# When loads, bank seeds and weight jobs are issued in a kernel of 518 hand-ordered steps

## The chip, the cores and the metric

The kernel runs on one core of a Trainium2 chip. The metric is the device time of one execution, in microseconds (us), the median of several runs.

## The reference

Two branches work on the same input x (2048 x 640) and are mixed by a gate. All sizes are float32.

```
g = sigmoid((x * gate_w).sum(-1))                      # one gate for each row
a, b = x @ dft_hid_re.T, x @ dft_hid_im.T              # 640 x 640 each
A = dft_seq_re @ a - dft_seq_im @ b                    # 2048 x 2048 each
h = x @ w1 + b1                                        # 640 x 1728
B = (h * tanh(softplus(h))) @ w2                       # Mish, then 1728 x 640
out = g * A + (1 - g) * B
```

## The kernel before, in words

**Arithmetic.** Every float32 operand is split into two rounded parts: ScalarE copies it to the high part (`rh` for moving operands, `wh` for weights), VectorE subtracts to get the low part (`rl`, `wl`). A product is three matmuls, high by high, high by low, low by high (`mm3`, all recorded at line 141; splits at line 125 for the copies of ScalarE and line 122 for the sums of VectorE). Blocks of 2 x 2 are multiplied with seven products in place of eight (Strassen-Winograd), so that many sums of operands, of weights and of results lie on VectorE, and partial results pass through DRAM or are copied back into a PSUM bank as the start of another sum. Such a copy is called a *seed* here (`preload`, `seed`, `take_y`: ScalarE `ps<-f`).

**Steps.** All the work of TensorE is cut into 518 steps, each of 6 to 25 matmuls of 128 x 512, in one list, `steps`: raw loads, preparations (`prep`: splits), matmuls, and a `post` that takes results out of the banks. In order they are: the stages on the sequence and the hidden dimension (steps 0 to 335), the dense stage x @ w1 (336 to 417) and the out stage with w2 (418 to 517). The dense stage begins at step `nd` = 336 with four pairs of remainder steps `r` (`dense_rest`, the last block of columns) and seven quad steps `q` (`dense_quads(0)`, one block of a second level of seven products) in an order written out by hand, `ORDER`; then `dense_first(0)` from `nm` = 351, `dense_quads(1)` from `nq` = 379, and `dense_first(1)` to step 417. A pair of column groups f, f+1 in `dense_first` takes steps p5, p6, p3, p7 and p4 for both: p5 opens bank "b", p6 adds to bank "a", into which a partial product that an earlier quad had stored to DRAM (`p1_...`) was loaded and seeded; p3 ends with a product of the odd column block, operand "dd", a difference of two tiles.

**One loop sets the order of everything** (lines 1346 to 1393). All engines but SP run their own queue in program order. For each step i the loop emits: the preparations of steps up to i + LEAD_D (6, in the dense stage; 7 elsewhere), and before them raw loads of steps up to AHEAD_D (6) further; step i's matmuls; stores that are due; step i's `post`; the events that were attached to step i with `at`; pieces of weight jobs; loads for further weight jobs. All loads and stores go through the one queue of SP, in this order; an entry that waits holds up those behind it. A raw load is issued early only while more than `spare(i)` buffers are free.

**Weight jobs** (splitting and summing blocks of weights, the gate rows, sums of x) stand in one list; `JOBS` gives its last part. A job's pieces are emitted after a step when a planner's account of VectorE's time is behind that of TensorE:

```
1385  while clock["dve"] < clock["pe"] + (SLACK_D if nd <= i < nm + D_END else SLACK if ("seq", "low", KH - 1) in done_jobs else SLACK_UP) and i >= wait_until and i not in quiet:
```

So SLACK_D (0.0) holds from step 336 up to nm + D_END, SLACK (-1.0) before and after it, in us. In the `quiet` steps (nd - 4 to nd + QUIET and nm - 7 to nm + QUIET_M) no piece is emitted, in the `no_load` steps (three before the out stage to NO_LOAD after its start) no job's loads. `need(key)` in a preparation forces all pieces up to that job at once. `XS_FIRST` and `FIRSTS` give the first step at which certain jobs may be loaded.

**Seeds.** `P_SEED`, `P_SEED_0`: the event, counted from its pair's p5, at which `dense_first` seeds a bank "a" (`_0`: the first pair of the first call); `P_LOAD`, `P_LOAD_0`: how many steps ahead its tile is loaded. `SEED_Q` and `P_Q_0`: the same for the banks of `dense_quads(1)`. `take_y` (line 638): the out stage's first banks are seeded with a negative partial y, in an event one step before that stage's step n, from a tile loaded at n - 6. `T0`: steps, counted from nm, to which the loads of operands s1, s2, s4, dd, s3 of `dense_first(0)` are attached; their split is prepared LEAD_D steps ahead of that. `E_LEAD` and `R1` place the splits of narrow operands of the quads and of a remainder step.

Of the kernel before, what the change touches and what calls it, by code (L numbers as in the profile page):

```python
# [23 lines left out]
EARLY = 3  # L24
LEAD = 7
LEAD_D = 6
AHEAD_D = 6
AHEAD = 6
SPARE = 3
SPARE_D = 2  # L30
SPARE_OUT = 5
SLACK = -1.0
SLACK_UP = 2.5
SLACK_D = 0.0
QUIET = 2
NR = 9
NFS = 22
NFX = 4
# [3 lines left out]
BACK = -17  # L42
NB = 3
NLOAD = 6
QUIET_M = -3
D_END = 7
ORDER = 'rrqrrqrrqqrqrqq'
Q_LEAD = 2
P_Q = 2
P_LOAD = 4  # L50
P_LOAD_0 = 3
P_SEED = 0
P_SEED_0 = -1
P3_LAG = 2
Q_LAG = 0
SEED_Q = 1
P_Q_0 = 4
NO_LOAD = 5
XS_FIRST = 179
XS_EACH = 8  # L60
T0 = (0, 5, 5, 8, 6)
T1 = (3, 3, 5, 5, 7, 10, 10)
QX_AT = -1
N_KEPT = 1
Q2_LEAD = 1
E_LEAD = 2
R0 = (3, 2)
R1 = (1, 3)
JOBS = 'q0 q1 q2 y20 y21 y22 y23 y24 y30 y31 t2 y32 y33 t3 y34 l0 t1 l1 t0 l2 t4 t5 c r l3 l4 l5'
FIRSTS = {'y20': 37, 'y34': 42, 'l0': 22, 't2': 0}  # L70

# [14 lines left out]
def fnet_mish_gate(ctx: ExitStack, tc: tile.TileContext, xn, xt, c_re, c_im, wd_re, wd_im,  # L88
# [35 lines left out]
    def copy(o, a, scale=1.0):  # L124
        nc.scalar.activation(o, a, AF.Copy, scale=scale)  # L125
# [38 lines left out]
    def at(i, fn):  # L164

        events.setdefault(i, []).append(fn)
# [14 lines left out]
    def simple(fn):  # L181
        def work(*a):
            fn(*a)
            return
            yield
        return work
# [6 lines left out]
    def fs_load(src):  # L193
        f = FS.get()
        nc.sync.dma_start(f[:src.shape[0]], src)
        return f
# [171 lines left out]
    class Problem:  # L368
# [269 lines left out]
        def take_y(self, name, t, d, n):  # L638

            at(n - 6, lambda: RAW.update({("y", d): fs_load(ysc[d][t])}))  # L640

            def put():
                f, ps = RAW.pop(("y", d)), psum.get()
                PS.setdefault(name, []).append(ps)
                copy(ps, f, -1.0)
                FS.put(f)
            at(n - 1, put)

        def y_load(self, i, t, *ds):
            for d in ds:  # L650
# [135 lines left out]
    def w2_job(name, g):  # L786
        W2C[name] = W.get()
        split(*W2C[name], g)
        FX.put(g)
# [19 lines left out]
    def x_split(key, f, keep=False):  # L809
        r = X[key] = R.get()  # L810
        split(r[0], r[1], f)
        if not keep:
            FS.put(f)
# [6 lines left out]
    def x_diff(key, a, b):  # L820
        f, g = RAW.pop(a), RAW.pop(b)
        tt(f, f, g, OP.subtract)
        FS.put(g)
        x_split(key, f)
# [87 lines left out]
    def x_sums(dst, a21, a22, a11, a12):  # L912
        s1 = FS.get()
        tt(s1, a21, a22, OP.add)
        store(dst("s1"), s1, s1)
        yield 1
        tt(a21, a11, a21, OP.subtract)
        store(dst("s3"), a21, a21)
        FS.put(a11)
        yield 1  # L920
        tt(a22, a22, a21, OP.subtract)
        store(dst("s2"), a22, a22)
        yield 1
        tt(a12, a12, a22, OP.subtract)
        store(dst("s4"), a12, a12)

    def x_sum_jobs():
# [3 lines left out]
        for n, (key, dst, srcs) in enumerate(todo):  # L931
            jobs.append(Job(key, lambda *f, dst=dst: x_sums(dst, *f), lambda srcs=srcs: [fs_load(v) for v in srcs], fs=5))
            jobs[-1].first = XS_FIRST + XS_EACH * n

# [22 lines left out]
    def dense_quads(q):  # L957
# [64 lines left out]
        def p1_loads(n, j, tp):  # L1022
            def go():
                for g in range(FP // 2):
                    assert id(qout[2 * g + j][tp]) not in unwritten
                    KEEP["c", 2 * g + j, tp] = fs_load(qout[2 * g + j][tp])
            at(n, go)
            takes[n] = takes.get(n, 0) + 3

        for b, x, w, d, post in (("b", "a12", "b21", (0, "d1", 0), lambda: snap("b", "q2")),  # L1030
# [19 lines left out]
            if x == "a12":  # L1050
                preps = [lambda: [need(k) for k in ["five"] * q + [("quad", q, g) for g in range(FP // 2)]]]
                if q:
                    at(n - SEED_Q, seed)
                    p1_loads(n - P_Q_0, 0, 0)
                    narrow_loads.extend((n + E_LEAD + i, (("xe", t), xt[t, KD - 1])) for t, i in ((0, 0), (2, 2)))
                    attach.append((n + E_LEAD, lambda: x_split(("d1", 0, 0), RAW[("xe", 0)], True)))
                    attach.append((n + E_LEAD + 2, lambda: x_split(("d1", 0, 1), RAW[("xe", 2)], True)))
                    attach.append((n + E_LEAD + 4, lambda: x_diff(("de", 0, 0), ("xe", 0), ("xe", 2))))
            if q and x in ("s1", "s2", "a22"):
# [8 lines left out]
    def dense_first(tp, end, ops):  # L1068
# [39 lines left out]
        def p1_load(f):  # L1108
            assert id(qout[f][tp]) not in unwritten
            KEEP["p1", f] = fs_load(qout[f][tp])  # L1110

        def seed(f):

            H["a", f] = psum.get()
            p1 = KEEP.pop(("p1", f))
            copy(H["a", f], p1)
            FS.put(p1)
# [9 lines left out]
        def parts(fp):  # L1127

            fa, fb, over = fp, fp + FP, fp == FP - 1

            def free(*names):
                if over:
                    x_free(*[(n, k, tp) for n in names for k in range(2 if n[0] != "d" else 1)])

            def p5_post():
                snap("p5", "b", fp)
                free("s1")

            def p6_post():
                snap("u2", "a", fp)  # L1140
                free("s2")

            def p3_post():
                o = add("b", "u2", fp)
                pop("b", fp)
                later(P3_LAG, lambda: out_act(fb, t1, o, o))
                free("s4", "dd")

            def p7_post():
                o = add("a", "p5", fp)  # L1150
                at(clock["step"] + 1, lambda: out_act(fb, t2, o, o))
                free("s3")

            def p4_post():
                ps = H.pop(("a", fp))

                def last():
                    out_act(fa, t2, FS.get(), ps)
                    psum.put(ps)
                at(clock["step"] + 2, last)  # L1160
                free("a22", "d2")
                if end:
                    W.put(*W1[fp])
                    if fp == FP - 1:
                        W.put(*T2B, *W5)

            return [
                ([lambda: need(("w1", fp))], sub(fp, [("b", "s1", at_cols(1, 0), True)], [("b", "d2", 1)]), p5_post),
                ([], sub(fp, [("a", "s2", t2_at(fp), False)]), p6_post),
                ([], sub(fp, [("b", "s4", at_cols(0, 2 * P), False)], [("b", "dd", 1)]), p3_post),  # L1170
                ([], sub(fp, [("a", "s3", at_cols(1, 2 * P), False)]), p7_post),
                ([], sub(fp, [("a", "a22", at_cols(0, 0), False)], [("a", "d2", 0)]), p4_post)]


        for fp in range(0, FP, 2):
            for j in range(2):
                f, n = fp + j, len(steps) + j
                if True:
                    i = n - (P_LOAD if tp or fp else P_LOAD_0)
                    at(i, lambda f=f: p1_load(f))  # L1180
                    takes[i] = takes.get(i, 0) + 1
                at(n + (P_SEED if tp or fp else P_SEED_0), lambda f=f: seed(f))
            p5, p6, p3, p7, p4 = zip(parts(fp), parts(fp + 1))
# [92 lines left out]

    for o in JOBS.split():
        if o[0] == "y":
# [7 lines left out]
        else:  # L1286
            jobs.append(Job("w2r", simple(lambda g: w2_job("r", g)), w2r_load, 1, 1))
        if o in FIRSTS:
            first_at[jobs[-1].key] = FIRSTS[o]
    sq[0].first(True)  # L1290
# [12 lines left out]
    nd = len(steps)  # L1303
    rests = [dense_rest(2, False, (0, 0)), dense_rest(3, False, (0, 0)), dense_rest(0, True, R0), dense_rest(1, True, R1, True)]
    rests = [r for r in rests for _ in range(2)]
    quads = dense_quads(0)
    for o in ORDER:
        next(quads if o == "q" else rests.pop(0))
    n0 = nm = len(steps)
    dense_first(0, False, [("s1", n0 + T0[0]), ("s2", n0 + T0[1]), ("s4", n0 + T0[2]), ("dd", n0 + T0[3]), ("s3", n0 + T0[4])])  # L1310
    nq = len(steps)
# [8 lines left out]
    narrow.update(range(nd, len(steps)))  # L1320
    quiet = set(range(nd - 4, nd + QUIET)) | set(range(nm - 7, nm + QUIET_M))
    n_dense = len(steps)
    no_load = set(range(n_dense - 3, n_dense + NO_LOAD))
    ou[0].first(ks=range(3))
# [16 lines left out]
    def spare(i, job=False):  # L1341

        return SPARE + (SPARE_D * job if i in narrow else (i >= n_dense) * SPARE_OUT) + sum(takes.get(i + j, 0) for j in range(5))

    li = ready = 0
    wait_until = 0
    for i in range(n_all):
        clock["step"] = i
        while ready < n_all and ready <= i + (LEAD_D if ready in narrow else LEAD):
            while li < len(loads) and loads[li][0] <= ready + (AHEAD_D if loads[li][0] in narrow else AHEAD):  # L1350
                n, (key, src) = loads[li]
# [30 lines left out]
        if not (jobs or loaded or running):  # L1382
            while FX.free:
                FS.put(FX.get()[:, :N])
        while clock["dve"] < clock["pe"] + (SLACK_D if nd <= i < nm + D_END else SLACK if ("seq", "low", KH - 1) in done_jobs else SLACK_UP) and i >= wait_until and i not in quiet:
            if running:
# [55 lines left out]
```

## Time and profile before

| | us |
|---|---|
| median of three runs | 863.79 (863.53 to 863.9) |
| the profiled execution | 863.96 |
| its span in the profile | 862.2 |
| TensorE busy (3757 matmuls) | 855.5 |
| VectorE busy | 739.1 |
| ScalarE busy | 501.6 |

Times in the profile count from the start of the span. PE is TensorE, PEld its weight loads, DVE VectorE, ACT ScalarE, SP (or SPq) the queue of DMA issues. A row of a timeline has the start, the duration, engine, line, operation, tiles written and read, their size and the number of instructions put together; in brackets stands how long the engine had been idle before and what released it. The duration of a matmul is modelled and overlaps the next one's, so the distance from start to start is what counts. A row of the windows has the stretch, its length, TensorE's busy time with its count of matmuls, the granted clock (1.00 is full), the share of DMA time and GB/s. A row of the chain has start, length, and what the last instruction of all was waiting for at that time, followed back.

### The profile page before, as it was taken

The page shows a single profiled execution, that of the slowest core. Times are in us where ns is not written, and L with a number is a line of the kernel's source. Part 1 is how long each engine was busy: PE and PEld are TensorE (multiplying, and loading weights), DVE is VectorE, ACT ScalarE, POOL GpSimd, SP SyncE. Part 2 cuts the span into 40 slices and gives each one's busy share as a digit, 9 for nine tenths or more (in the row PEclk, how much of TensorE's full clock was granted, in tenths as well). Part 3 has the DMA queues.
Part 4 walks back from the last instruction along what each step waited for, and adds up shares of the span by engine and source line. Part 5 has one row for each costly group of instructions (what it writes and reads, how often), then busy time and mean ns, then how long its engine had stood idle before and what let it go on. Part 6 is the DMA issues. An engine that isn't in the chain of part 4 may idle for free.

```text
span 862.2 us, 12400 instructions
## 1 busy us (share of the span) xinstructions
PE 855.5 (99%) x3757; PEld 706.1 (82%) x3757; DVE 739.1 (86%) x1296; ACT 501.6 (58%) x933; POOL 0.2 (0%) x4
## 2 busy tenths in 40 slices
PE   9999999999999999999999999999999999999998
PEld 7888888888888888888888888778888887888886
DVE  6999988889879779898998996956877988998993
ACT  6756645464554544657656766857865857442532
POOL 0000000000000000000000000000000000000000
PEclk9999999999999999999999999999999999999999
DMA  9976748786859899989586979787999997595952
GB/s 349 327 239 229 258 132 307 276 278 217 298 202 296 277 353 310 367 262 361 194 264 201 329 247 346 272 277 226 342 326 381 333 367 234 191 318 174 348 194 109
DMA packets 130915, 237.35 MB, mean 275 GB/s; under 512 B 15008, under 2 KB 19872, under 8 KB 130848
## 3 DMA queue, kind: packets, MB, share of 16 engines
q1 hardware_dynamic: 130416, 235.91, 79.7%
q8 instruction: 29, 0.48, 0.2%
q10 hardware_dynamic: 432, 0.66, 0.2%
q14 instruction: 38, 0.31, 0.1%
HBM read 186.16 MB, written 50.35 MB: 274 GB/s over the span
## 4 chain that ended last, share of the span: by engine, by line
PE 94%; DVE 2%; ACT 2%; DMA 1%; issue 1%; SPq 0%; DVEq 0%
PE ps L141 94%; DVE f L122 1%; ACT f L125 1%; ACT wh L125 1%; DMA p<-f 1%; DVE rl L122 1%; DVE wl L122 1%; DMA act<-f 0%; DMA f<-p 0%; ACT rh L125 0%; ACT f L831 0%; DVE f L874 0%; DVE fx L122 0%; ACT ps L125 0%; ACT f L879 0%
## 5 line engine op out<-in xcount | busy, mean ns | idle before, releaser
L141 PE MATMUL ps<-rh,wh 128*128 128x512 f32 (+1 forms) x1067 | 414.3, 390 | 0.7 <-ACT ps L125 0.5
L141 PE MATMUL ps<-rh,wl 128*128 128x512 f32 x1051 | 408.0, 389 | 0.0
L141 PE MATMUL ps<-rl,wh 128*128 128x512 f32 x1050 | 407.6, 389 | 0.0
L125 ACT ACTIVATE rh<-f 128x512 fp32r<-128x512 f32 (+1 forms) x427 | 256.0, 626 | 181.4 <-DVE f L122 87.7
L122 DVE TENSOR_TENSOR rl<-f,rh 128x512 fp32r<-128x512 f32 x425 | 277.8, 685 | 52.7 <-ACT rh L125 45.6
L141 PEld LDWEIGHTS ps<-rh,wh 128*128 128x128 f32 x1067 | 200.4, 188 | 43.3 <-ACT ps L125 0.9
L122 DVE TENSOR_TENSOR f<-f,f 128x512 f32<-128x512 f32 (+1 forms) x337 | 225.3, 674 | 9.1 <-ACT f L125 1.3
L141 PEld LDWEIGHTS ps<-rh,wl 128*128 128x128 f32 x1051 | 197.3, 188 | 41.1
L141 PEld LDWEIGHTS ps<-rl,wh 128*128 128x128 f32 x1050 | 197.1, 188 | 40.7
L125 ACT ACTIVATE f<-ps 128x512 f32<-128x512 f32 (+1 forms) x153 | 88.6, 594 | 73.8 <-PE ps L141 68.4
L125 ACT ACTIVATE wh<-f 128x512 fp32r<-128x512 f32 (+3 forms) x188 | 85.3, 495 | 52.4 <-DVE f L122 49.2
L122 DVE TENSOR_TENSOR wl<-f,wh 128x512 fp32r<-128x512 f32 (+3 forms) x188 | 92.7, 526 | 20.5 <-ACT wh L125 20.1
L141 PE MATMUL ps<-wh,wh 128*128 128x512 f32 x197 | 77.0, 391 | 1.3 <-ACT wh L125 1.2
L141 PE MATMUL ps<-wl,wh 128*128 128x512 f32 x192 | 74.8, 390 | 0.2 <-DVE wl L122 0.2
L141 PE MATMUL ps<-wh,wl 128*128 128x512 f32 x191 | 74.4, 389 | 0.0
L122 DVE TENSOR_TENSOR f<-ps,f 128x512 f32<-128x512 f32 x83 | 53.8, 681 | 13.3 <-PE ps L141 13.2
L141 PEld LDWEIGHTS ps<-wh,wh 128*128 128x128 f32 x197 | 37.0, 188 | 10.1 <-ACT wh L125 2.0
L141 PEld LDWEIGHTS ps<-wl,wh 128*128 128x128 f32 x192 | 36.0, 188 | 7.9 <-DVE wl L122 0.5
L141 PEld LDWEIGHTS ps<-wh,wl 128*128 128x128 f32 x191 | 35.9, 188 | 7.4
L125 ACT ACTIVATE ps<-f 128x512 f32<-128x512 f32 x49 | 27.7, 594 | 17.7 <-DVE f L122 12.9
L122 DVE TENSOR_TENSOR wl<-fx,wh 128x640 fp32r<-128x640 f32 (+4 forms) x44 | 28.5, 654 | 6.6 <-ACT wh L125 6.6
L831 ACT ACTIVATE f<-f,b1s 128x512 f32<-128x512 f32 x36 | 24.5, 716 | 13.0 <-DVE f L122 13.0
(37 smaller groups left out, 167.5 us busy)
## 6 DMA issues: line engine op xcount, KB each, us to landing
f<-in_c_re_dram SPq DMA_DIRECT2D x128, 256.0 KB, 4.5
f<-in_c_im_dram SPq DMA_DIRECT2D x128, 256.0 KB, 4.7
f<-act SPq DMA_DIRECT2D x94, 256.0 KB, 5.1
f<-u SPq DMA_DIRECT2D x80, 256.0 KB, 4.4
f<-in_xt_dram SPq DMA_DIRECT2D x59, 256.0 KB, 5.1
act<-f SPq DMA_DIRECT2D x52, 256.0 KB, 5.1
u<-f SPq DMA_DIRECT2D x40, 256.0 KB, 4.3
f<-y SPq DMA_DIRECT2D x34, 256.0 KB, 5.3
```

The costliest lines, as they stand in the source:

```text
L122: nc.vector.tensor_tensor(o, a, b, op=op)
L125: nc.scalar.activation(o, a, AF.Copy, scale=scale)
L141: nc.tensor.matmul(ps, a, b, start=start, stop=stop, skip_group_check=True)
L831: nc.scalar.activation(o[rows], src[rows], AF.Mish, bias=b1s[rows, f:f + 1])
```

## The change

No operation is added or taken away; constants that place things are changed, and `take_y` gets one of its own.

- AHEAD_D: raw loads of the dense stage three steps ahead of their preparation, not six. SPARE_OUT: one buffer less is kept free in the out stage.
- SLACK -1.5 and not -1.0, QUIET, QUIET_M, D_END: the weight jobs' budget and the steps without pieces; the stretch in which SLACK_D holds ends before step nm - 1 = 350 and not before nm + 7 = 358; the first quiet stretch ends before nd - 3 and not before nd + 2, the second before nm - 2 and not before nm - 3.
- ORDER: the last remainder pair's second step comes ahead of quad step s4, not behind it. Before, steps 346 to 350 are r, q (s4), r, q (s3), q (a22); after, r, r, q (s4), q (s3), q (a22).
- P_LOAD 3 (was 4), P_SEED_0 0 (was -1): tiles of `dense_first` are loaded three steps ahead; its first pair of banks is seeded one event later.
- Y_SEED 2: `take_y` seeds two steps ahead of its stage, not one. SEED_Q 3 (was 1) and P_Q_0 7 (was 4): the second quad's seeds and their loads, two and three steps earlier.
- T0's last 8 (was 6): operand s3 two steps later, behind dd. E_LEAD 1, R1 (1, 4): a narrow split one step earlier, half of a remainder operand's split one step later.
- NO_LOAD, XS_FIRST, FIRSTS, JOBS: loads of jobs sooner after the out stage's start; sums of x 16 steps earlier; `l0` 8 steps earlier; t2 and t3 further ahead in the list, l3 last.

```diff
-AHEAD_D = 6
+AHEAD_D = 3
-SPARE_OUT = 5
-SLACK = -1.0
+SPARE_OUT = 4
+SLACK = -1.5
-QUIET = 2
+QUIET = -3
-QUIET_M = -3
-D_END = 7
-ORDER = 'rrqrrqrrqqrqrqq'
+QUIET_M = -2
+D_END = -1
+ORDER = 'rrqrrqrrqqrrqqq'
-P_LOAD = 4
+P_LOAD = 3
-P_SEED_0 = -1
+P_SEED_0 = 0
-SEED_Q = 1
-P_Q_0 = 4
-NO_LOAD = 5
-XS_FIRST = 179
+Y_SEED = 2
+SEED_Q = 3
+P_Q_0 = 7
+NO_LOAD = 1
+XS_FIRST = 163
-T0 = (0, 5, 5, 8, 6)
+T0 = (0, 5, 5, 8, 8)
-E_LEAD = 2
+E_LEAD = 1
-R1 = (1, 3)
-JOBS = 'q0 q1 q2 y20 y21 y22 y23 y24 y30 y31 t2 y32 y33 t3 y34 l0 t1 l1 t0 l2 t4 t5 c r l3 l4 l5'
-FIRSTS = {'y20': 37, 'y34': 42, 'l0': 22, 't2': 0}
+R1 = (1, 4)
+JOBS = 'q0 q1 q2 y20 y21 y22 t2 y23 y24 y30 y31 y32 t3 y33 y34 l0 t1 l1 t0 l2 t4 t5 c r l4 l5 l3'
+FIRSTS = {'y20': 37, 'y34': 42, 'l0': 14, 't2': 0}
...
-            at(n - 1, put)
+            at(n - Y_SEED, put)
```

## The prediction

> **What bounds the kernel now.** I read the page first, then the windows of TensorE, the chain, and around each piece of the chain that is not TensorE the timeline.
>
> ```profile
> span 862.2 us, 12400 instructions
> ...
> PE 855.5 (99%) x3757; PEld 706.1 (82%) x3757; DVE 739.1 (86%) x1296; ACT 501.6 (58%) x933; POOL 0.2 (0%) x4
> ...
> ```
>
> TensorE is busy 99% of the span. Busy is a modelled figure, so the pitch decides: how far apart matmuls start where nothing stops them.
>
> ```profile
> 568.00:683.00 115.00, 115.00 (x509) 1.00 0.89 309
> ```
>
> 509 matmuls in 115.0 us are 0.226 us each at a granted clock of 1.00. The program issues the same 3757 matmuls after the change, so 0.226 us each is the floor, and only what makes TensorE stand still can be won. The Trainium skill, page "TensorE: Matmul & The Clock Gate", section "Back-to-back issue gap", gives about 131 ns for a sustained matmul of 512 columns; by that, matmuls would need some 492 us (an estimate) and VectorE would set the time. This trace does not agree: 226 ns.
>
> ```profile
> 554.11 5.37 DMA p<-f
> ...
> 559.54 2.76 DMA f<-p
> ...
> 567.20 108.24 PE ps L141 x476
> ...
> 713.12 145.37 PE ps L141 x640
> ```
>
> In the chain the last 145 us are TensorE alone. What lies before it shows where the stream broke; the starts of TensorE's matmuls give all five places with a pitch over 0.24 us after the first microseconds:
>
> ```profile
> 554.03 0.39 PE L141 MATMUL ps<-rh,wl 128*128 128x512 f32 x1
> 555.17 0.47 PE L141 MATMUL ps<-wh,wh 128*128 128x512 f32 x1 [0.75 <-ACT wh L125]
> 555.48 0.40 PE L141 MATMUL ps<-wl,wh 128*128 128x512 f32 x1
> ...
> 562.51 0.39 PE L141 MATMUL ps<-wh,wl 128*128 128x512 f32 x1
> 562.98 0.50 PE L141 MATMUL ps<-wh,wh 128*128 128x512 f32 x1
> ...
> 565.62 0.39 PE L141 MATMUL ps<-rh,wl 128*128 128x512 f32 x1
> 566.47 0.50 PE L141 MATMUL ps<-wh,wh 128*128 128x512 f32 x1 [0.46 <-ACT wh L125]
> 567.20 0.50 PE L141 MATMUL ps<-wl,wh 128*128 128x512 f32 x1 [0.22 <-DVE wl L122]
> 567.53 0.40 PE L141 MATMUL ps<-wh,wl 128*128 128x512 f32 x1
> ...
> 683.20 0.39 PE L141 MATMUL ps<-wh,wl 128*128 128x512 f32 x1
> 683.75 0.50 PE L141 MATMUL ps<-rh,wh 128*128 128x512 f32 x1 [0.16 <-DVE f L122]
> ...
> 712.23 0.39 PE L141 MATMUL ps<-rh,wl 128*128 128x512 f32 x1
> 713.12 0.50 PE L141 MATMUL ps<-rh,wh 128*128 128x512 f32 x1 [0.50 <-ACT ps L125]
> ```
>
> Loss is the distance of starts less 0.226 per matmul. **S1** (step 350, last of the first quad's): 1.45 - 0.45 = 1.0 us, with the slower restart (0.31) in it. **S2** (step 354): 0.47 - 0.23 = 0.24, and 0.1 for a restart as in S1 and S3: 0.35. **S3** (the dd products of step 355): 1.91 - 0.68 = 1.23. **S4** (step 416): 0.55 - 0.23 + 0.1 = 0.42. **S5** (step 430): 0.89 - 0.23 + 0.1 = 0.76. Together 3.76 us, 0.44% of the time. No edit can win more; whatever it does elsewhere is hidden beside TensorE or costs.
>
> **The change part by part.** All engines issue the same instructions; only their order changes.
>
> **S1.** Step 350 writes the bank that step 349 filled, and waits for VectorE's sum out of it.
>
> ```profile
> 550.30 1.21 DVE L122 TENSOR_TENSOR wl<-f,wh 128x128 fp32r<-128x128 f32 x3
> 551.43 1.88 DVE L122 TENSOR_TENSOR f<-ps,f 128x512 f32<-128x512 f32 x3
> ...
> 552.42 0.60 ACT L125 ACTIVATE f<-ps 64x512 f32<-64x512 f32 x1 [1.06 <-PE ps L141]
> ...
> 553.23 0.73 DVE L874 SCALAR_TENSOR_TENSOR f<-ps,b1s,f 64x512 f32<-64x512 f32 x1
> ...
> 554.35 1.87 DVE L122 TENSOR_TENSOR f<-ps,f 128x512 f32<-128x512 f32 x3
> ```
>
> The first of the three sums at 554.35 ends at 555.02 (1.87 less two pitches of 0.6), and TensorE goes on at 555.17. VectorE is late because the remainder step's copy (552.42) and its addition (553.23) come just before, behind weight pieces (550.30) that a `need` forced. ORDER puts the remainder step ahead of quad s4 (steps 347 and 348 change places): its copy then starts at about 550.35, as early as 552.42 less the nine matmuls of s4 (2.04). Addition 551.1 to 551.8, s4's three sums from 551.75 at 0.6, so the first sum of step 349 is at 553.55 to 554.23. Step 350 is due at 554.03 + 0.23 = 554.26. The jobs' earlier budget (SLACK, QUIET_M, D_END, JOBS) takes the forced pieces away from this place. S1 keeps 0 to 0.2: I take -0.9. If the pieces stayed, 1.2 us of VectorE work would lie ahead of these sums and S1 would be what it was; both ends: 0 and -1.0.
>
> **S2 and S3.**
>
> ```profile
> 562.32 0.60 ACT L125 ACTIVATE ps<-f 128x512 f32<-128x512 f32 x1 [1.36 <-DMA f<-p]
> ...
> 565.78 0.63 ACT L125 ACTIVATE wh<-f 128x512 fp32r<-128x512 f32 x1 [1.23 <-DVE f L122]
> ```
> ```profile
> 565.07 0.69 DVE L122 TENSOR_TENSOR f<-f,f 128x512 f32<-128x512 f32 x1
> 566.45 0.69 DVE L122 TENSOR_TENSOR wl<-f,wh 128x512 fp32r<-128x512 f32 x1 [0.69 <-ACT wh L125]
> ```
>
> S2: the seed of step 354's bank (562.32) waits for a partial product that was stored (554.11, 5.37 us) and loaded again (559.54, 2.76 us). Its data come from s4's sums, which end about 553.3 before and about 553.6 after, but the first of them, the one that is needed, at 552.4. SP no longer has the six-step-ahead loads in front of that store; issued at 552.5 and landing in 2.8 us, as the load did, the store is over at 555.3 and the load at 558.1. With 5.4 us for each instead, the load lands at 563.3 and S2 grows by 1.0. P_SEED_0 moves the seed one event later, behind step 352's copy (about 560.6 to 561.2), so ScalarE itself sets it: 561.1 to 561.7, against 561.78 due. I take -0.3, between -0.35 and +1.0.
>
> S3: difference, rounding and remainder of dd (565.07, 565.78, 566.45) hang on ScalarE, which stood 1.36 us for the seed, and on job pieces between. With S1 and S2 gone ScalarE arrives 1.4 us earlier, and T0 sends s3's two splits behind dd, not ahead. In the order of the queues dd's three instructions come at 562.2, 562.9 and 563.6 to 564.25; due are 564.5 and 564.7. I take -1.15, bounds 0 and -1.23.
>
> **S4 and S5.**
>
> ```profile
> 683.01 0.68 DVE L122 TENSOR_TENSOR f<-ps,f 128x512 f32<-128x512 f32 x1
> ```
> ```profile
> 711.35 1.22 ACT L125 ACTIVATE f<-ps 128x512 f32<-128x512 f32 x2 [0.18 <-PE ps L141]
> 712.47 1.63 ACT L125 ACTIVATE ps<-f 128x512 f32<-128x512 f32 x3
> ```
>
> S4 waits for the sum at 683.01, in a VectorE queue without a pause, whose order from step 403 to 417 the change leaves alone: 0. S5: five seeds stand behind two copies out of the bank that ends at step 429. Y_SEED puts them one event earlier, ahead of those copies; they start about 2 us sooner and the bank is ready 1 us before it is due. What is late next is the two copies (5 x 0.6 = 3 us later), whose bank is used again only several steps on, and the y loads, issued at the same event as before and so with four steps of nine matmuls (8.1 us) in place of five. The out stage's other early seed, at step 416, has as much and nothing waiting for it now. -0.76, or 0 if the loads are late.
>
> **The rest, at nothing.** AHEAD_D, P_LOAD, SEED_Q, P_Q_0, E_LEAD, R1, NO_LOAD, SPARE_OUT, QUIET, XS_FIRST, FIRSTS and the jobs' order move DMAs, copies and splits that lie beside TensorE. An operand is split six steps before its use, 8 us or more (six matmuls a step are 1.36 us). Weight jobs come about 13 steps earlier up to step 300, where TensorE never waits; one, low 3 of the out stage, is now forced by its `need` at step 436, seven steps (14 us) ahead of its use. If that cover is gone:
>
> ```profile
> f<-p SPq DMA_DIRECT2D x24, 256.0 KB, 5.4
> ...
> f<-xs SPq DMA_DIRECT2D x16, 256.0 KB, 5.0
> ```
> ```profile
> ACT rh L125 <- DMA f<-in_xt_dram: 1.6, 1, 1.6
> ```
>
> Three steps are 4.1 to 6.1 us, a load has a median of 5.0. So ScalarE, whose queue is in order, can stand up to 5.0 - 4.1 = 0.9 us at a split, 1.6 at the worst (seen once before). The Trainium skill, page "DMA: Bandwidth & Descriptors", section "Anatomy of one DMA — SWDGE (gpsimd) path", fits 2.0 us plus bytes at 436 GB/s, 2.6 us for such a tile as an estimate; by it nothing would stand, by the row it could. The row, with other transfers queued, decides.
>
> **Sum:** -0.9 - 0.3 - 1.15 - 0.76 = -3.1. The profiled execution took 863.96 (862.2 of span and 1.76 around it), 0.17 over the median 863.79; so 860.85 by it, 860.7 as a median.
>
> **The rivals.**
> *A, only the plain moves work.* S5 goes and S1 mostly, but S2 and S3 stay, since their DMA chain runs at 5.4 us: 863.8 - 0.76 - 0.9 = 862.1, or 863.0 if S1 stays too. For it: the store in front took 5.37. Against: it was issued in a burst of three behind other transfers.
> *B, the change doesn't do what it says.* SP's order is also set by free buffers; loads "three steps ahead" may go out when they did, and one new wait may eat S5's gain: 863.3 to 864.3. Against: S5 and ORDER need no buffer.
> *C, slower.* Three steps are too few: from the point where a load lands over 0.5 us after ScalarE reaches its split, the copies and seeds behind it in ScalarE's queue are late, and 19 groups of operands pass that queue between steps 346 and 417. If six to eight of them cost 0.9 each and the rest goes as forecast: 860.7 + 5.4 = 866.1 to 860.7 + 7.2 = 867.9. For it: the 5.0 us row. Against: ScalarE is busy 58%, and seeds are copied two steps or more ahead of their use, at least 2.7 us.
>
> **How the numbers follow.** The forecast (860.0 to 861.7) has 0.64, A 0.14 (0.06 of it under 862.06), B 0.10, C 0.12. A measurement of this kernel tells 0.2% from no change, 1.73 us. Faster 0.64 + 0.06 = 0.70, same 0.08 + 0.10 = 0.18, slower 0.12. The range runs from 863.8 - 3.76 - 0.1 = 859.9, everything gone, to 863.6, which takes in A and a part of B and leaves out about 0.17.
>
> **What would show it.** In the profile after: a chain that is TensorE from the start to 0.5 us before the step-416 break, no distance of starts over 0.25 us near 554, 562, 565 and 710, the one at about 680 (683.2 less what was won before) still 0.55, and a span of 859.1. Wrong would be a ScalarE line waiting for `DMA f<-xs` or `DMA f<-p` for over 1 us with TensorE standing behind it (A or C), or breaks at places that had none, the quad steps after 594 above all.

## The result, and the profile after

The changed kernel takes 860.95 us (median of 7 runs, 860.29 to 861.5) where the kernel before takes 863.9 (7 runs beside them, 863.4 to 864.18). The ratio is 0.9966, 95% interval 0.9955 to 0.9978: 2.95 us faster, against 3.1 forecast. The profiled execution took 861.26 us with a span of 859.5.

Of the chain, its shares and its two long pieces in the changed kernel (line numbers are one higher than before, L142 for L141):

```profile
PE 99%; ACT 0%; DVE 0%; issue 0%
```
```profile
0.77 672.75 PE ps L142 x2955
...
681.82 173.96 PE ps L142 x766
```

The chain is TensorE from the start to 8 us ahead of one break, and TensorE again from there. That break and the two small ones that are left, as starts of matmuls:

```profile
554.47 0.39 PE L142 MATMUL ps<-rh,wl 128*128 128x512 f32 x1
554.72 0.47 PE L142 MATMUL ps<-rh,wh 128*128 128x512 f32 x1
555.03 0.40 PE L142 MATMUL ps<-rl,wh 128*128 128x512 f32 x1
```
```profile
562.32 0.48 PE L142 MATMUL ps<-rh,wh 128*128 128x512 f32 x1
562.64 0.40 PE L142 MATMUL ps<-rl,wh 128*128 128x512 f32 x1
```
```profile
681.27 0.39 PE L142 MATMUL ps<-rh,wl 128*128 128x512 f32 x1
681.82 0.50 PE L142 MATMUL ps<-wh,wh 128*128 128x512 f32 x1 [0.16 <-DVE f L123]
682.16 0.40 PE L142 MATMUL ps<-wl,wh 128*128 128x512 f32 x1
```

Counted as in the prediction (distance of starts less 0.226 a matmul), S1 has 0.11 left, S2 0.09, S3 and S5 nothing, S4 0.43. The sum fell from 3.78 to 0.68 with a new 0.05 at step 385: 3.1 us won. The spans differ by only 2.7, because this execution lost 0.4 us more in its first microseconds. The start of the same group of matmuls, before and after:

```profile
7.30 0.85 PE L141 MATMUL ps<-rh,wh 128*128 128x512 f32 x3
```
```profile
7.72 0.63 PE L142 MATMUL ps<-rh,wh 128*128 128x512 f32 x2
```

What freed S1 to S3, on ScalarE and then VectorE of the changed kernel:

```profile
550.82 0.60 ACT L126 ACTIVATE f<-ps 64x512 f32<-64x512 f32 x1 [1.38 <-PE ps L142]
...
561.66 0.60 ACT L126 ACTIVATE ps<-f 128x512 f32<-128x512 f32 x1
563.47 1.67 ACT L126 ACTIVATE wh<-f 128x512 fp32r<-128x512 f32 x3 [1.22 <-DVE f L123]
```
```profile
551.45 0.74 DVE L875 SCALAR_TENSOR_TENSOR f<-ps,b1s,f 64x512 f32<-64x512 f32 x1 [1.86 <-ACT f L126]
552.11 3.66 DVE L123 TENSOR_TENSOR f<-ps,f 128x512 f32<-128x512 f32 x6
...
562.75 0.68 DVE L123 TENSOR_TENSOR f<-f,f 128x512 f32<-128x512 f32 x1
```

VectorE now waits 1.86 us for the remainder's copy, where it came late before; the six sums follow without a weight piece between them. Less the 0.42 us of the start, the rows stand where the prediction put them: copy 550.4 (550.35), addition 551.0 (551.1), seed 561.2 (561.1), difference of dd 562.3 (562.2). The seed waits for no DMA.

Not every sign that the prediction named came out. The 0.55 at step 416 is there; but two distances near 554 and 562 are 0.31 and 0.32 where none was to be over 0.25, and one of the quad steps after 594 has a new break, of 0.05. They cost 0.25 us together.

### The profile page after: what moved, and what is told of

It is laid out like the page before. It is cut to its first block, busy times and chain, and to the rows that moved or that the text cites. A ratio compares the mean times of both kernels' runs of the same rounds, so it can differ in the third digit from the quotient of the medians.

```text
span 859.5 us, 12393 instructions
## 1 busy us (share of the span) xinstructions
PE 854.8 (99%) x3757; PEld 706.5 (82%) x3757; DVE 739.2 (86%) x1296; ACT 499.0 (58%) x933; POOL 0.2 (0%) x4
## 4 chain that ended last, share of the span: by engine, by line
PE 99%; ACT 0%; DVE 0%; issue 0%
PE ps L142 99%; DVE f L123 0%; ACT f L126 0%; ACT rh L126 0%; ACT f L832 0%; ACT wh L126 0%; DVE rl L123 0%; DVE wl L123 0%
## 5 line engine op out<-in xcount | busy, mean ns | idle before, releaser
L142 PE MATMUL ps<-rh,wh 128*128 128x512 f32 (+1 forms) x1065 | 413.5, 390 | 0.0
L142 PE MATMUL ps<-rl,wh 128*128 128x512 f32 x1048 | 407.1, 389 | 0.0
L142 PE MATMUL ps<-rh,wl 128*128 128x512 f32 x1047 | 406.4, 389 | 0.0
L126 ACT ACTIVATE rh<-f 128x512 fp32r<-128x512 f32 x417 | 249.4, 627 | 169.5 <-DVE f L123 86.8
L123 DVE TENSOR_TENSOR rl<-f,rh 128x512 fp32r<-128x512 f32 x416 | 272.5, 685 | 43.7 <-ACT rh L126 41.7
L142 PEld LDWEIGHTS ps<-rh,wh 128*128 128x128 f32 x1065 | 200.1, 188 | 42.1 <-ACT wh L126 0.3
L142 PEld LDWEIGHTS ps<-rl,wh 128*128 128x128 f32 x1048 | 197.1, 188 | 40.8
L142 PEld LDWEIGHTS ps<-rh,wl 128*128 128x128 f32 x1047 | 196.5, 188 | 41.0
L123 DVE TENSOR_TENSOR f<-f,f 128x512 f32<-128x512 f32 (+1 forms) x329 | 219.4, 673 | 11.6 <-DMA f<-in_xt_dram 4.0
L126 ACT ACTIVATE wh<-f 128x512 fp32r<-128x512 f32 (+3 forms) x195 | 89.2, 499 | 58.3 <-DVE f L123 54.9
L123 DVE TENSOR_TENSOR wl<-f,wh 128x512 fp32r<-128x512 f32 (+3 forms) x194 | 96.4, 531 | 16.7 <-ACT wh L126 16.2
L142 PE MATMUL ps<-wh,wh 128*128 128x512 f32 x199 | 77.6, 390 | 0.2 <-DVE f L123 0.2
L142 PE MATMUL ps<-wh,wl 128*128 128x512 f32 x195 | 75.9, 389 | 0.0
L142 PE MATMUL ps<-wl,wh 128*128 128x512 f32 x194 | 75.5, 389 | 0.0
L123 DVE TENSOR_TENSOR f<-ps,f 128x512 f32<-128x512 f32 x88 | 56.7, 682 | 8.1 <-PE ps L142 6.5
L142 PEld LDWEIGHTS ps<-wh,wh 128*128 128x128 f32 x199 | 37.4, 188 | 8.4 <-DVE f L123 0.8
L142 PEld LDWEIGHTS ps<-wh,wl 128*128 128x128 f32 x195 | 36.6, 188 | 7.7
L142 PEld LDWEIGHTS ps<-wl,wh 128*128 128x128 f32 x194 | 36.4, 188 | 7.5
```

Of the source, the lines that this page charges most:

```text
L123: nc.vector.tensor_tensor(o, a, b, op=op)
L142: nc.tensor.matmul(ps, a, b, start=start, stop=stop, skip_group_check=True)
```

## The experiments

The theory of the prediction was a list, one cause for each break. The runs below took it apart. The nine constants of the weight jobs were changed only together (the *budget* below), and P_LOAD, P_SEED_0, SEED_Q, P_Q_0, E_LEAD and R1 were never changed alone. Ratios are against the kernel before on the same chip at the same time (its median was 863.91 beside the first four runs and beside the next four, 863.69 beside the last four); losses are of the profiled execution, in us.

| | S1 | S2 | S3 | S4 | S5 | other places | median | ratio (95%) |
|---|---|---|---|---|---|---|---|---|
| before | 1.0 | 0.36 | 1.23 | 0.43 | 0.77 | | 863.9 | |
| changed | 0.11 | 0.09 | 0 | 0.43 | 0 | 0.05 | 860.95 | 0.9966 (0.9955 to 0.9978) |
| b_yseed | 0.83 | 0.10 | 1.24 | 0.44 | 0 | | 862.98 | 0.9992 (0.9983 to 1.0) |
| b_order | 1.68 | 0 | 0.36 | 0.44 | 0.77 | | 863.68 | 1.0003 (0.9995 to 1.0012) |
| b_jobs | 0.36 | 0.02 | 0.57 | 0.44 | 0.77 | | 862.05 | 0.9982 (0.9973 to 0.9991) |
| a_jobs | 1.25 | 0.75 | 1.05 | 0.44 | 0 | 342: 0.76, 346: 1.36, 353: 1.1 | 866.51 | 1.0031 (1.0019 to 1.0044) |
| b_ahead3 | 4.8 | 1.2 | 1.2 | 0.44 | 0.77 | 342: 0.4, 379: 1.9 | 870.11 | 1.0075 (1.006 to 1.0091) |
| a_ahead6 | 0.11 | 0.09 | 0 | 0.44 | 0 | | 860.9 | 0.9963 (0.9951 to 0.9975) |
| a_ahead1 | 1.6 | 0.09 | 8.0 | 0.6 | 0 | 343 to 346: 2.4, 385: 0.8, 394: 4.3 | 876.45 | 1.014 (1.0125 to 1.0155) |
| a_quiet | 0.11 | 0.09 | 0 | 0.80 | 0 | 381 to 385: 2.1 | 861.7 | 0.9975 (0.9966 to 0.9985) |
| b_min | 0.36 | 0 | 0.67 | 0.44 | 0 | | 861.57 | 0.9975 (0.9966 to 0.9983) |
| a_order | 0.35 | 0.09 | 0.03 | 0.44 | 0 | 385: 0.09 | 861.38 | 0.9972 (0.9961 to 0.9983) |
| a_jobs6 | 1.86 | 0.18 | 0.23 | 0.44 | 0 | 385: 0.10 | 862.34 | 0.9984 (0.9975 to 0.9994) |
| a_late | 0.11 | 0.09 | 0 | 0 | 0 | 385: 0.07 | 860.62 | 0.9965 (0.9953 to 0.9978) |

**b_yseed**: the kernel before with the out stage's early seeds moved.

```diff
-            at(n - 1, put)
+            at(n - 2, put)
```

> The kernel before with one line changed: the out stage's early seeds two steps ahead of their stage, not one. Theory (S5 is the order of ScalarE's queue alone): the break near 712 goes, the four others stay, 863.9 - 0.76 = 863.1. Rival (the y loads are not there in time, or the two copies that now come 3 us later hold a bank): a break near 712 or a new one within 10 us after it, 863.9 or more.

862.98. The break near 712 went and nothing came for it. ScalarE's row shows why: all five seeds now stand together, done at 712.2, where the first of them began at 712.47 before.

```profile
709.53 2.67 ACT L125 ACTIVATE ps<-f 128x512 f32<-128x512 f32 x5
```

S5 was the order of one queue, as forecast.

**b_order**: the kernel before with the new order alone.

```diff
-ORDER = 'rrqrrqrrqqrqrqq'
+ORDER = 'rrqrrqrrqqrrqqq'
```

> The kernel before with the new ORDER alone: the remainder step ahead of quad step s4. Theory (breaks S1 to S3 stand in a row behind one chain, and the forced weight pieces lead it): S1 shrinks from 1.0 to 0.4 or 0.5, because the pieces forced at step 346 now stand in front of the remainder's addition; what it wins is lost at S2, whose store still leaves SP at about 554, so that S2 grows to 0.8 or so: 863.5 to 864.0. Rival (ORDER is what removes S1 and the later breaks follow): S1 at 0.1, S2 and S3 under 0.2, 861.6.

863.68 (862.81 to 865.71), no difference that can be measured. The time came out as the theory said, but by other breaks: S1 grew to 1.68 and S2 was gone. ScalarE and then VectorE of this run:

```profile
550.95 0.59 ACT L125 ACTIVATE f<-ps 64x512 f32<-64x512 f32 x1 [0.60 <-DMA actr<-f]
```
```profile
549.28 1.22 DVE L122 TENSOR_TENSOR wl<-f,wh 128x128 fp32r<-128x128 f32 x3
551.57 0.74 DVE L874 SCALAR_TENSOR_TENSOR f<-ps,b1s,f 64x512 f32<-64x512 f32 x1 [1.07 <-ACT f L125]
552.24 1.87 DVE L122 TENSOR_TENSOR f<-ps,f 128x512 f32<-128x512 f32 x3
554.03 0.54 DVE L122 TENSOR_TENSOR wl<-fx,wh 128x384 fp32r<-128x384 f32 x1
554.50 1.87 DVE L122 TENSOR_TENSOR f<-ps,f 128x512 f32<-128x512 f32 x3
```

With the remainder's addition ahead of the three sums of s4, all of them wait for ScalarE's copy (1.07 us of VectorE idle), which itself comes behind weight pieces and a 0.60 us wait for a store to land; and the piece of 0.54 at 554.03 still stands ahead of the sum that step 350 wants; that sum ends at about 555.2 where 553.7 was due. By these rows the order is no gain while weight pieces stand at that place.

**b_jobs**: the kernel before with the weight jobs' constants alone.

```diff
-SPARE_OUT = 5
-SLACK = -1.0
+SPARE_OUT = 4
+SLACK = -1.5
-QUIET = 2
+QUIET = -3
-QUIET_M = -3
-D_END = 7
+QUIET_M = -2
+D_END = -1
-NO_LOAD = 5
-XS_FIRST = 179
+NO_LOAD = 1
+XS_FIRST = 163
-JOBS = 'q0 q1 q2 y20 y21 y22 y23 y24 y30 y31 t2 y32 y33 t3 y34 l0 t1 l1 t0 l2 t4 t5 c r l3 l4 l5'
-FIRSTS = {'y20': 37, 'y34': 42, 'l0': 22, 't2': 0}
+JOBS = 'q0 q1 q2 y20 y21 y22 t2 y23 y24 y30 y31 y32 t3 y33 y34 l0 t1 l1 t0 l2 t4 t5 c r l4 l5 l3'
+FIRSTS = {'y20': 37, 'y34': 42, 'l0': 14, 't2': 0}
```

> The kernel before with the new planner constants of the weight jobs alone (SLACK, QUIET, QUIET_M, D_END, NO_LOAD, SPARE_OUT, XS_FIRST, JOBS, FIRSTS); ORDER, AHEAD_D, the seeds and T0 as before. Theory (the budget leads the chain: with no pieces forced at step 346 VectorE and SP are free): S1 falls to 0.3 or 0.4, S2 goes, S3 falls to 0 to 0.4, S4 and S5 stay: 863.9 - 2.0 = 861.9, give or take 0.4. Rival (ORDER and AHEAD_D remove S1 and S2): S1 and S2 stay, 863.4 to 863.9.

862.05, as the theory had it, though S3 kept 0.57 where 0 to 0.4 was expected. The store for S2 left SP at 549.27 and its load at 552.59, without AHEAD_D. SP of the kernel before, then of this run:

```profile
550.08 0.94 SPq L190 DMA_DIRECT2D fx<-in_w1a_dram  x2
```
```profile
549.27 1.59 SPq L1367 DMA_DIRECT2D p<-f  x3
552.59 0.32 SPq L195 DMA_DIRECT2D f<-p  x1
...
555.56 4.12 SPq L190 DMA_DIRECT2D fx<-in_w1a_dram  x2
```

Three things changed for that store. Before, two loads of weights stood ahead of it, and SP went on from transfer to transfer until it issued it at 554.11, 2.0 us after the sum to be stored was ready (552.1, the first of the three at 551.43); here they come behind it, and it leaves as soon as its sum is there. The sum itself comes 2.1 us sooner, counted from the same start, because no weight pieces stand ahead of it on VectorE. And the store takes 3.3 us to land, not 5.37.

**a_jobs**: the changed kernel with the same constants set back (the diff above reversed).

> The changed kernel with the planner constants of before, all else as changed. Theory (the budget leads the chain): pieces are forced at step 346 again, S1 is 0.4 or 0.5, the store for S2 leaves SP at 553.5 or later and S2 is 0.3 to 1.0, S3 0 to 0.5: 862.0 to 862.8. Rival (ORDER, AHEAD_D and T0 suffice): S1 to S3 under 0.2 each, 861.0.

866.51: the theory's direction, but some four times its size, and slower than the kernel before. ScalarE and SP show what the theory had left out:

```profile
558.07 0.63 ACT L126 ACTIVATE wh<-f 128x512 fp32r<-128x512 f32 x1 [2.90 <-DMA f<-xs]
```
```profile
549.34 0.59 SPq L1368 DMA_DIRECT2D act<-f  x1
552.00 0.81 SPq L191 DMA_DIRECT2D fx<-in_w1a_dram  x2
552.85 1.85 SPq L1359 DMA_DIRECT2D f<-xs  x4
```

SP stood from 549.9 to 552.0 at a load of weights, whose buffers the forced pieces had not given back. The operand tiles (`xs`), now three steps ahead, are queued behind it and land after ScalarE has reached their split; it stands 2.90 us with the seeds behind it. That is rival C of the prediction, at work in half of the change. The next three runs change that distance alone.

**b_ahead3**: the kernel before with that one constant.

```diff
-AHEAD_D = 6
+AHEAD_D = 3
```

> The kernel before with AHEAD_D = 3 alone. Theory (three steps are too few while SP is held up by weight loads that wait for buffers of the forced pieces: the tiles of s2 and s4 are then issued behind those weight loads and land after ScalarE reaches their split): ScalarE stands 1 to 3 us for the xs tiles at about 555, S1 stays, S2 and S3 together grow by 1.3, S4 and S5 stay: 865.2, between 864.6 and 866.0. Rival (the loss of the run without the new budget came from other constants): 863.5 to 864.2, or faster if loads that are later free SP for the store of S2: 863.0.

870.11. The mechanism was right, the price far too small, and S1, which was to stay, took most of it (4.8). The same load of weights holds SP until 552.39; ScalarE stands 1.63 us for `xs`, after 1.60 for VectorE, TensorE 3.05 us before step 350, and there is a second such place (step 379), where ScalarE stood 2.63 us.

```profile
552.39 0.81 SPq L190 DMA_DIRECT2D fx<-in_w1a_dram  x2
553.25 1.85 SPq L1358 DMA_DIRECT2D f<-xs  x4
```
```profile
556.32 0.63 ACT L879 ACTIVATE f<-f 64x512 f32<-64x512 f32 x1 [1.60 <-DVE f L874]
558.58 1.37 ACT L125 ACTIVATE wh<-f 128x512 fp32r<-128x512 f32 x2 [1.63 <-DMA f<-xs]
```
```profile
613.15 0.63 ACT L125 ACTIVATE rh<-f 128x512 fp32r<-128x512 f32 x1 [2.63 <-DMA f<-q1s]
```
```profile
557.49 0.76 PE L141 MATMUL ps<-wh,wh 128*128 128x512 f32 x1 [3.05 <-DVE f L122]
558.05 0.63 PE L141 MATMUL ps<-wl,wh 128*128 128x512 f32 x1
```

The rest of the price comes behind the last row: after the standstill the matmuls from 558.05 on start 0.43 us apart, not 0.226 (the last section has more on it).

**a_ahead6**: the changed kernel with `AHEAD_D = 6`.

> The changed kernel with AHEAD_D = 6 again. Theory (with the new budget the loads are held by free buffers, not by steps; SP's order near step 349 differs by one load): the same breaks as in the changed kernel, 861.0 give or take 0.3. Rival (the loads in front of the store are what made S2): S2 of 0.3 or more, and S3 behind it, 861.5 to 862.2.

860.9, the same breaks to 0.01 us, but without the 0.05 at step 385. With the new jobs' constants the store for S2 leaves SP at 552.63, against 552.81 in the changed kernel. AHEAD_D is worth nothing here.

**a_ahead1**: the changed kernel with `AHEAD_D = 1`.

> The changed kernel with loads only one step ahead of their preparation. Theory (rival C of the prediction is a real mechanism with a threshold between three steps and one): ScalarE stands for loads of operands in several places by 1 to 3 us, the seeds and copies behind it are late, breaks near 562 and after 594: 863 to 867. Rival (a preparation six steps ahead of its use covers it): 861.0, no new break over 0.2.

876.45, beyond the theory's 867. So with the pieces out of the way the margin ends between three steps and one. The longest break, at step 355, hangs on a load of x for dd that SP issued at 568.88, behind six stores. VectorE stood 5.80 us for it:

```profile
572.61 0.69 DVE L123 TENSOR_TENSOR f<-f,f 128x512 f32<-128x512 f32 x1 [5.80 <-DMA f<-in_xt_dram]
```

Two matmuls start 5.1 us apart there, and 3.0 us at step 394; both breaks cost more than that (8.0 and 4.3), because the matmuls behind them start 0.43 us apart.

**a_quiet**: the changed kernel with seven more quiet steps ahead of S4.

```diff
     n_dense = len(steps)
+    quiet |= set(range(n_dense - 9, n_dense - 2))
```

> The changed kernel with seven more quiet steps, 409 to 415, so that about 3 us of VectorE's weight pieces (low 2) move behind step 416. Theory (S4 is VectorE's queue alone): the break at step 416 goes and nothing comes for it, 861.0 - 0.43 = 860.5. Rival (the pieces are missed later, at the forced low 2 and low 3): a break between steps 418 and 445, 861 or more.

861.7 (9 runs, 860.73 to 863.58, the profiled one the slowest): the theory failed. S4 rose to 0.80. The order of the instructions shows that top 0 is needed by the preparation of step 418, so that it and the last piece of low 1 were forced at step 411, ahead of that preparation. The breaks at 381 to 385 are of this profiled execution: up to step 408 the program is that of the changed kernel. In the chain they go back to a load of the second quad's seeds that took 6.82 us:

```profile
604.66 6.82 DMA f<-p
```

**b_min**: the kernel before with the constants of b_jobs, the seeds of b_yseed and

```diff
-T0 = (0, 5, 5, 8, 6)
+T0 = (0, 5, 5, 8, 8)
```

> The kernel before with three parts of the change: the weight jobs' constants, T0 and the early seeds of the out stage; ORDER, AHEAD_D, P_LOAD, P_SEED_0, SEED_Q, P_Q_0, E_LEAD and R1 as before. Theory (the jobs' budget, the order of dd and s3 and the place of five seeds are the whole gain): S1 at 0.36 as with the budget alone, S2 and S3 under 0.1, S5 gone, S4 0.43: 863.9 - 0.65 - 0.35 - 1.2 - 0.76 = 860.9. Rival (the other constants carry a part of it): S3 stays near 0.6, 861.3 or more.

861.57: here the rival was right. S3 stays at 0.67, no less than in b_jobs without T0. VectorE shows why, in b_jobs and then in b_min:

```profile
562.71 0.69 DVE L122 TENSOR_TENSOR f<-f,f 128x512 f32<-128x512 f32 x1
...
564.70 0.42 DVE L122 TENSOR_TENSOR fx<-fx,fx 128x256 f32<-128x256 f32 x1
```
```profile
562.34 0.42 DVE L122 TENSOR_TENSOR fx<-fx,fx 128x256 f32<-128x256 f32 x1
...
563.93 0.68 DVE L122 TENSOR_TENSOR f<-f,f 128x512 f32<-128x512 f32 x1
```

T0 did move s3's two splits behind the difference of dd (`f<-f,f`). But four sums of a weight job (`fx<-fx,fx` is the first), which come behind dd in b_jobs, took their place ahead of it. Less the 1.1 us by which this execution started later, dd comes 0.1 us later than in b_jobs, as S3 does.

**a_order**: the changed kernel with the old ORDER.

> The changed kernel with the old ORDER. Theory (with the pieces gone from that place ORDER is worth only the rest of S1): S1 0.3 to 0.4 and not 0.1, nothing else moves: 861.2. Rival (ORDER is what removes S1): S1 at 1.0, 861.8 or more.

861.38. S1 is 0.35 and S3 0.03: ORDER is worth 0.24 us of S1 on top of the rest, and is not what ends S3. These two runs differ at S3 by one seed. ScalarE of b_min, then of a_order:

```profile
560.77 0.62 ACT L125 ACTIVATE ps<-f 128x512 f32<-128x512 f32 x1
561.29 0.54 ACT L125 ACTIVATE wh<-fx 128x384 fp32r<-128x384 f32 x1
```
```profile
560.56 0.54 ACT L126 ACTIVATE wh<-fx 128x384 fp32r<-128x384 f32 x1
561.21 0.60 ACT L126 ACTIVATE f<-ps 128x512 f32<-128x512 f32 x1
561.70 0.60 ACT L126 ACTIVATE ps<-f 128x512 f32<-128x512 f32 x1
```

In b_min the second seed stands ahead of the weight piece (561.29) on which VectorE's chain to dd hangs; with P_SEED_0 one event later it stands behind it, and the piece comes at 560.56. The difference of dd follows at 563.93 in the one and 563.20 in the other; 0.2 of that is the start, 0.5 is the time of one seed.

**a_jobs6**: a_jobs with `AHEAD_D = 6` as well.

> The changed kernel with the planner constants of before and AHEAD_D = 6: the earlier run with these constants, but the loads six steps ahead again. Theory (what made that run 866.5 were late loads behind weight loads; the rest of it is the forced pieces): ScalarE's wait of 2.9 us for xs tiles goes, breaks at 353 and 354 with it, 863.0, between 862.3 and 864.2. Rival (the forced pieces and R1 alone did it): 866 again.

862.34. With the loads ahead of the weights' loads again, 4.2 us of a_jobs go, and the breaks at 342, 346 and 353 with them; what stays is S1, 1.86, as b_order would have it.

**a_late**: the changed kernel with the out stage's first six preparations later and five quiet steps.

```diff
     n_dense = len(steps)
+    quiet |= set(range(n_dense - 7, n_dense - 2))
...
-        while ready < n_all and ready <= i + (LEAD_D if ready in narrow else LEAD):
+        while ready < n_all and ready <= i + (LEAD_D if ready in narrow else 4 if n_dense <= ready < n_dense + 6 else LEAD):
```

> The changed kernel with the out stage's first six steps prepared four steps ahead and not seven, and five quiet steps, 411 to 415, so that nothing is forced: before the sum that S4 waits for, VectorE and ScalarE have three splits each and about 2 us less to do. Theory (S4 is the fill of these two queues): the break at step 416 goes, nothing comes for it, 861.0 - 0.43 = 860.5. Rival (the work is missed later): a break between steps 418 and 445, 861 or more.

860.62. S4 is gone, and from the first product to the last the chain is a single piece of TensorE:

```profile
4.57 849.76 PE ps L142 x3748
```

By the order of the instructions the later preparations did it, not the quiet steps: in steps 411 to 417 the changed kernel has no weight piece either.

In the runs its 0.43 us can't be told from the changed kernel (0.9965 and 0.9966, intervals 0.0023 and more wide, of different groups); the trace shows it.

## Why the prediction was right, and where its reasons were not

- *TensorE's pitch is the floor, five breaks are all there is to win*: right. The medians follow the sums of breaks within 0.8 us, but for a_ahead1 and a_quiet, where one execution's breaks were not those of the median.
- *S1 to 0 to 0.2*: right in size (0.11). The share of each edit was wrong. The prediction let ORDER do the work and the budget clear the way; alone, the budget takes 0.64 of it (b_jobs) and ORDER adds 0.7 (b_order); ORDER's own part, once the pieces are gone, is 0.24 (a_order). With the pieces in place S1 was to stay what it was; it grew. Which of the budget's nine constants does it is open.
- *S2, SP no longer has the six-step-ahead loads in front of the store*: wrong cause, right times (less the start, the store left at 552.4, as against 552.5, and S2 has 0.09 left). AHEAD_D at 6 gives the same S2 (a_ahead6), and S2 goes without AHEAD_D (b_jobs). What the budget takes away from the store is two loads of weights ahead of it on SP and the weight pieces ahead of its sum on VectorE; how much each weighs was not measured apart.
- *S3, T0 sends s3 behind dd*: wrong step, right size. The budget alone takes about half of it (0.57 left in b_jobs), and T0 with the budget no more (0.67 left in b_min), since pieces of a weight job fill the place. The rows of b_min and a_order point to P_SEED_0, which the prediction used for S2 alone; no run changed it alone, so that is argued and not shown.
- *S4 left alone*: right. That VectorE's queue alone sets it was too narrow; the chain behind it goes back over ScalarE, and it went when three splits on each engine came later (a_late), not when pieces did (a_quiet).
- *S5, -0.76*: right, by its own mechanism (b_yseed).
- *The sum, -3.1*: 3.1 by the breaks. The times that the prediction read from the order of the queues held, which is why the sizes came out; but two of its four terms, S2 and S3, rest on edits that did not do it, and that other edits of the same change did is luck.
- *The rest at nothing*: right in this sum, and wrong as a reason. The price put on a lost cover, 0.9 to 1.6 us of ScalarE at a split, was 2.90 in a_jobs, and AHEAD_D alone makes the kernel before 6.2 us slower. Rival C asked whether three steps are enough for a load; what decides is what stands ahead of that load in SP's queue.

## What to carry to other kernels

Where one engine runs at its pitch, list every break in its starts, follow each back, and the sum is the most that reordering can win. Edits to such an order are not a sum of their own effects: the same load distance cost nothing, 4 us or 6 us, by whether the one in-order DMA queue was held up by a load waiting for a buffer. To ask which edit did it, set each back alone and make each alone; here the two answers differ. ORDER alone makes S1 0.7 us longer, and with the rest in place it makes it 0.24 shorter. AHEAD_D alone costs 6.2 us, and nothing with the rest in place.

## What the runs showed of the hardware

After a standstill of TensorE the clock falls. The windows of b_ahead3 around its 3.4 us between two starts (columns as before; the granted clock is the third figure from the end):

```profile
557.40:561.00 3.60, 3.51 (x9) 0.55 1.04 395
561.00:566.00 5.00, 5.00 (x24) 1.00 0.71 247
```

And those of a_ahead1 behind 5.1 us and behind 3.0 us between two starts:

```profile
574.00:580.00 6.00, 5.99 (x13) 0.50 0.39 128
...
659.00:662.20 3.20, 3.18 (x8) 0.51 0.54 171
```

For about 3 to 6 us matmuls start some 0.43 us apart: in b_ahead3 the eight distances from 557.49 on are 3.38 us, 1.6 more than at 0.226. Behind 2.04 us between two starts (step 379 of b_ahead3) there was nothing of it. The Trainium skill, page "TensorE: Matmul & The Clock Gate", section "What's actually happening", has this gate, half speed after an idle window of about 3.4 us that runs freely. The traces agree with the half speed; 3.0 us between two starts, less than that window, was already enough.

An execution also starts slowly: from 1.32 on matmuls are 0.43 us apart, in every run, though the granted clock reads 1.00 there. When that ends differs. The same three matmuls in the changed kernel, still in part slow, and in a_late:

```profile
6.02 1.17 PE L142 MATMUL ps<-rl,wh 128*128 128x512 f32 x3
```
```profile
5.37 0.86 PE L142 MATMUL ps<-rl,wh 128*128 128x512 f32 x3
```

The distances fall to about 0.23 us at 3.8 us in a_late and at 6.8 us in the changed kernel, whose programs are the same up to there. The Trainium skill, page "TensorE: Matmul & The Clock Gate", section "What you observe", lets this end vary by 0.5 us from run to run; these two traces, 3.0 us apart, do not agree. The group of matmuls that starts at 7.30 before and at 7.72 after starts at 6.76 in a_late: 0.96 us between executions, a third of this change's gain, and reason enough to count breaks and not spans.
